# A gated mix of linear attention and a token MLP: phi(q) by token rows, normalised on GpSimd and VectorE and turned by DMA, with six y tiles held

## The chip, the core and the metric

The kernel runs on one core of one Trainium2 chip. TensorE (PE in the profile) multiplies matrices, ScalarE (ACT), VectorE (DVE) and GpSimd (POOL) do the rest, and SyncE (SP) issues nearly all DMAs, in order, from one queue. Times are microseconds of device time of one launch, and the metric is the median over runs.

## What is computed

Inputs are bf16. x has 2048 tokens of 512 features, there are 32 heads of 16, and F is 1792.

```python
def _A_ref(x, wqkv, wo):                      # linear attention
    q, k, v = ...                             # (x @ wqkv), by head
    phi = lambda t: jnp.where(t > 0, t + 1, jnp.exp(t)) + 1e-6
    pq, pk = phi(q), phi(k)
    kv = jnp.einsum("bhsd,bhse->bhde", pk, v)
    z = jnp.einsum("bhsd->bhd", pk)
    num = jnp.einsum("bhqd,bhde->bhqe", pq, kv)
    den = jnp.einsum("bhqd,bhd->bhq", pq, z)[..., None] + 1e-6
    o = num / den
    return ... @ wo                           # heads side by side again

def _B_ref(x, w1, b1, w2, b2):                # MLP over the tokens
    h = _layernorm(x, axis=-1)
    u = _gelu(jnp.einsum("bsd,sf->bdf", h, w1) + b1)
    y = jnp.einsum("bdf,fs->bds", u, w2) + b2
    return ...                                # turned back to (tokens, features)

g = _sigmoid((x * gate_w).sum(-1, keepdims=True))
return g * _A_ref(A_x, A_wqkv, A_wo) + (1 - g) * _B_ref(B_x, ...)
```

The kernel uses A_x for both halves.

## The kernel before

Tokens lie in 16 tiles of 128 (t), features in 4 blocks of 128 (j or k), F in 14 blocks, and tokens also in 4 chunks of 512 (c). A matmul takes a 128x128 block as weights and a 128x512 block as data, into one of the eight PSUM banks of the tag "bank". The helpers mm and load (lines 73 and 126) hold every matmul and every DMA in program order on its engine, and pin does so for the others. In the profile all matmuls therefore have line 75 and all SP DMAs line 127.

The stages, in TensorE's order:

- accA: the first seven F blocks of x normalised times w1, while x and w1 come in and VectorE does the layer norm. gelu goes to ScalarE.
- kacc and Gps: k by token tile, phi(k) as pk, and G = x^T phi(k), which stands for kv before v's weights are applied. SP has loaded xT, x turned, with 16 DMA transposes (line 155). VectorE adds up zacc, the sum of phi(k) over 16 rows of each partition's tokens, split into z_hi and z_lo in bf16.
- The block loop (line 438), b = 0 to 6: each block has sixteen accB matmuls for one of the other seven F blocks. Block 0 then has kv_blocks and z_cols, which sums z over the partitions with eight matmuls of one column and lays it out by head in Z32. Block 1 has w2_blocks, which joins kv and wo to W2sb. Blocks 0 to 3 end with 3, 4, 4 and 5 q groups (line 352): each makes phi(q) turned, features on the partitions and 512 tokens along the row, straight into pqT. The gelus of blocks 0 to 3 run after the last phi; four accB banks are held until then. After block 3 VectorE has the last four gate sums, and after block 4 comes den (line 416): 16 matmuls of pqT by Z32, a reciprocal of 128x512 on VectorE, a store to rd_dram.
- Then SP reads 1/den back 16 times, repeated over each head's 16 rows (rex, line 500), and VectorE multiplies pqT by it in place (line 502). load_w2(1), the second half of w2 in two DMAs, is issued behind those reads. The first half, load_w2(0), was issued before the block loop.
- y and a: a y tile is 14 matmuls of w2 by uT for one token tile. An a tile is 4 matmuls of pqT by W2sb. ScalarE scales a to ga (line 480, three buffers), VectorE adds c1 times y to it into ot (line 489, four buffers), and SP stores ot. The first HOLD = 4 y tiles are all made before the first a tile, and wait in their banks. Tiles 0 to 7 read the first half of w2 and tiles 8 to 15 the second.

phi is one exp on ScalarE and two instructions on VectorE (lines 289 to 301).

Of the kernel before, what the change touches and what calls it, by code (L numbers as in the profile page):

```python
# [8 lines left out]
ACT = mybir.ActivationFunctionType  # L9
ALU = mybir.AluOpType  # L10
AX = mybir.AxisListType
BF16 = mybir.dt.bfloat16
FP32 = mybir.dt.float32
# [3 lines left out]
def kernel(  # L17
# [13 lines left out]
    nc = tc.nc  # L31
    P = nc.NUM_PARTITIONS
    EPS = 1e-5
    PHI_EPS = 1e-6
    DEN_EPS = 1e-6
    HEAD = 16
# [3 lines left out]
    S, D = X.shape  # L40
    F = B_w1.shape[1]
    NT = S // P
    ND = D // P
    NF = F // P
    SC = 512
    NSC = S // SC
# [16 lines left out]
    work = ctx.enter_context(tc.tile_pool(name="work", bufs=3))  # L63
    dpool = ctx.enter_context(tc.tile_pool(name="dpool", bufs=1, space=bass.MemoryType.DRAM))
    psum = ctx.enter_context(tc.tile_pool(name="psum", bufs=8, space=bass.MemoryType.PSUM))

    def ptile(shape, dt, name):
        return persist.tile(shape, dt, name=name, tag=name)

    def bank(name):  # L70
        return psum.tile([P, SC], FP32, name=name, tag="bank")

    def mm(o, lhsT, rhs, start, stop, **kw):
        tc.keep_in_program_order(
            nc.tensor.matmul(o, lhsT=lhsT, rhs=rhs, start=start, stop=stop, **kw)  # L75
        )

    xr = ptile([P, NT, D], BF16, "xr")
    xh = ptile([P, NT, D], BF16, "xh")
    xT = ptile([P, ND, S], BF16, "xT")  # L80
    wq_sb = ptile([P, ND, D], BF16, "wq_sb")
# [3 lines left out]
    pqT = ptile([P, ND, S], BF16, "pqT")  # L85
    uT = ptile([P, NF, D], BF16, "uT")
    G_sb = ptile([P, ND, D], BF16, "G_sb")
    kvbdT = ptile([P, ND, P], BF16, "kvbdT")
    Z32 = ptile([P, ND, 32], BF16, "Z32")
    W2sb = ptile([P, ND, D], BF16, "W2sb")  # L90
    mask = ptile([P, P], BF16, "mask")
    maskH = ptile([P, 8], BF16, "maskH")
    ident = ptile([P, P], BF16, "ident")
    gw_b = ptile([P, D], BF16, "gw_b")
    b_rows = ptile([NF + NT, P], BF16, "b_rows")
# [8 lines left out]
    c1 = ptile([P, NT], FP32, "c1")  # L104
    c2 = ptile([P, NT], FP32, "c2")
    warm = ptile([P, 256], BF16, "warm")
    ones1 = ptile([P, 1], BF16, "ones1")
    zacc = ptile([P, D], FP32, "zacc")
    z_hi = ptile([P, D], BF16, "z_hi")
    z_lo = ptile([P, D], BF16, "z_lo")  # L110
    zcol_sb = ptile([P, ND], FP32, "zcol_sb")
    rden_sb = ptile([P, SC], BF16, "rden_sb")
    eps_t = ptile([P, 1], FP32, "eps_t")
    den_eps_t = ptile([P, 1], FP32, "den_eps_t")
    den_sb = ptile([P, SC], FP32, "den_sb")

    nc.vector.memset(warm[:], 1.0)
    nc.vector.memset(eps_t[:], EPS)
# [5 lines left out]
    pin = tc.keep_in_program_order  # L124

    def load(o, i, eng=None, **kw):
        pin((eng or nc.sync).dma_start(out=o, in_=i, **kw))  # L127
# [24 lines left out]
    for c in range(NSC):  # L152
        for j in range(ND):
# [3 lines left out]
                transpose=True,  # L157
# [6 lines left out]
    for j in range(ND):  # L164
# [10 lines left out]
        out=mask[:], in_=mask[:], compare_op=ALU.is_gt, fill=1.0,  # L175
        base=1 - HEAD, pattern=[[-HEAD, 8], [0, HEAD]], channel_multiplier=1,
    )
    nc.gpsimd.affine_select(
        out=mask[:], in_=mask[:], compare_op=ALU.is_ge, fill=0.0,
        base=0, pattern=[[-HEAD, 8], [0, HEAD]], channel_multiplier=1,  # L180
    )
    nc.gpsimd.memset(maskH[:], 0.0)
    nc.gpsimd.affine_select(
        out=maskH[:], in_=maskH[:], compare_op=ALU.is_gt, fill=1.0,
        base=1 - HEAD, pattern=[[-HEAD, 8]], channel_multiplier=1,
    )
    nc.gpsimd.affine_select(
        out=maskH[:], in_=maskH[:], compare_op=ALU.is_ge, fill=0.0,
        base=0, pattern=[[-HEAD, 8]], channel_multiplier=1,
    )  # L190
    nc.gpsimd.memset(Z32[:], 0.0)
    nc.gpsimd.memset(ones1[:], 1.0)
    nc.gpsimd.memset(den_eps_t[:], DEN_EPS)


    warm_ps = bank("warm_ps")
# [55 lines left out]
    def gate(t):  # L252
        junk = work.tile([P, D], BF16, name="junk", tag="junk", bufs=2)
        tc.keep_in_program_order(
            nc.vector.tensor_tensor_reduce(  # L255
                out=junk[:], in0=xr[:, t, :], in1=gw_b[:], scale=1.0, scalar=0.0,
                op0=ALU.mult, op1=ALU.add, accum_out=gpre[:, t : t + 1],
            )
        )

    GATE_A = 12
# [27 lines left out]
    def phi(o, acc):  # L289
        e = work.tile([P, SC], BF16, name="e", tag="e", bufs=4)  # L290
        pin(nc.scalar.activation(out=e[:], in_=acc[:], func=ACT.Exp))  # L291
        pin(
            nc.vector.tensor_scalar(  # L293
                out=e[:], in0=e[:], scalar1=1.0, scalar2=PHI_EPS, op0=ALU.min, op1=ALU.add
            )
        )
        pin(
            nc.vector.scalar_tensor_tensor(  # L298
                out=o, in0=acc[:], scalar=0.0, in1=e[:], op0=ALU.max, op1=ALU.add
            )  # L300
        )
# [44 lines left out]
    def mlp1_block(j):  # L346
        acc = bank("accB")
        for t in range(NT):
            mlp1(acc, w1B, (j - NFA) * P, t, t == NT - 1)
        return acc  # L350

    def q_group(c, j):
        qacc = bank("qacc")
        for k in range(ND):
            mm(qacc[:], wq_sb[:, k, j * P : (j + 1) * P], xT[:, k, c * SC : (c + 1) * SC],
               k == 0, k == ND - 1)
        phi(pqT[:, j, c * SC : (c + 1) * SC], qacc)

    def z_cols():
        zcol_ps = bank("zcol_ps")  # L360
        for j in range(ND):
            mm(zcol_ps[:, j : j + 1], z_hi[:, j * P : (j + 1) * P], ones1[:], True, False)
            mm(zcol_ps[:, j : j + 1], z_lo[:, j * P : (j + 1) * P], ones1[:], False, True)
        pin(nc.vector.tensor_copy(out=zcol_sb[:], in_=zcol_ps[:, :ND]))
        for j in range(ND):
            pin(
                nc.vector.tensor_scalar_mul(
                    out=Z32[:, j, 8 * j : 8 * j + 8], in0=maskH[:], scalar1=zcol_sb[:, j : j + 1]
                )
            )  # L370

    def kv_blocks():
        kvps = bank("kvps")
# [18 lines left out]
    def w2_blocks():  # L392
        w2ps = [bank("w2ps") for _ in range(ND)]
        for j in range(ND):
            for p in range(0, P, 32):
                r = (p + 32 * j) % P
                mm(w2ps[j][p : p + 32, :], kvbdT[r : r + 32, j, p : p + 32],
                   wo_sb[r : r + 32, j, :], True, True, tile_position=(r, p))
        for j in range(ND):
            evict(W2sb[:, j, :], w2ps[j][:], j)  # L400
# [10 lines left out]
    load_w2(0)  # L411


    rd_dram = dpool.tile([P, SC], BF16, name="rd_dram", tag="rd_dram")

    def den():
        denps = bank("denps")
        for j in range(ND):
            for c in range(NSC):
                mm(denps[32 * c : 32 * c + 32, :], Z32[:, j, :], pqT[:, j, c * SC : (c + 1) * SC],  # L420
                   j == 0, j == ND - 1, tile_position=(0, 32 * c))
        pin(
            nc.scalar.activation(
                out=den_sb[:], in_=denps[:], func=ACT.Identity, bias=den_eps_t[:], scale=1.0
            )
        )
        with nc.allow_low_precision(reason="1/den in bf16 as the operands of the product"):
            pin(nc.vector.reciprocal(out=rden_sb[:], in_=den_sb[:]))
        load(rd_dram[:], rden_sb[:])

    QB = 4
    qlist = [(c, j) for c in range(NSC) for j in range(ND)]
    n_q = [3, 4, 4, 5]
    qi = 0
    waiting = []
    for b in range(NFA):
        acc = mlp1_block(NFA + b)
        waiting.append((acc, NFA + b))  # L440
        if b == 0:
            kv_blocks()
            z_cols()
        if b == 1:
            w2_blocks()
        if b < QB:
            for _ in range(n_q[b]):
                q_group(*qlist[qi])
                qi += 1
        if b >= QB - 1:  # L450
            for a, j in waiting:
                gelu(a, j)
            waiting = []
        if b == QB - 1:
            for t in range(GATE_A, NT):
                gate(t)
        if b == QB:
            den()
    assert qi == len(qlist)


    pin(nc.scalar.activation(out=gth[:], in_=gpre[:], func=ACT.Tanh, scale=0.5))
# [30 lines left out]
        )  # L493
        load(o_view[:, t, d0:d1], ot[:, d0:d1])

    for c in range(NSC):
        for j in range(ND):
            rex = work.tile([P, SC], BF16, name="rex", tag="rex", bufs=8)
            r_src = rd_dram[32 * c + 8 * j : 32 * c + 8 * j + 8, :]
            load(rex[:], r_src.unsqueeze(1).to_broadcast([8, HEAD, SC]))  # L500
            pin(
                nc.vector.tensor_tensor(  # L502
                    out=pqT[:, j, c * SC : (c + 1) * SC],
                    in0=pqT[:, j, c * SC : (c + 1) * SC], in1=rex[:], op=ALU.mult,
                )
            )

    load_w2(1)

    HOLD = 4  # L510
    held = []
    for t in range(HOLD):
        yps = bank("yps")
        y_mm(yps, t, 0, D)
        held.append(yps)
    for t in range(HOLD):
        ga = a_mm(t)
        finish(t, held[t], ga, 0, D)
    for t in range(HOLD, NT):
        ga = a_mm(t)  # L520
# [39 lines left out]
```

## Time and profile before

| | |
|---|---|
| median of 3 runs | 165.72 us (165.0 to 166.07) |
| the profiled execution | 165.5 us, of it a span of 163.8 us from the first instruction to the last |
| granted TensorE clock | 1.000 of full |
| q groups (qacc) on PE | 62.68 to 87.26 us, between the accB blocks |
| y and a tiles on PE | from 98.55 us to the end |
| DVE waits for ACT's exp (line 293) | 7.6 us in 3 times, the longest 3.1 |
| DVE's ot (line 489) waits for an output store | 7.0 us, once |
| first rex product (line 502) to the last, on DVE | 100.97 to 113.76 us |

The profile names a group of instructions by line, engine, operation and tiles (written tile <- read tiles), with the shapes. The timeline merges instructions of one kind that follow one another, with the start, the length, and the number. An idle time stands in brackets with what ended it. Matmuls overlap: one of 128x512 is shown as 379 ns long, but they start 216 ns apart.

### The profile page before, as it was taken

Reading aid. Unit: us, or ns where it says so; the run is one execution under the profiler, and the core shown is the slowest. Engines: PE = TensorE matmul, PEld = TensorE weight load, DVE = VectorE, ACT = ScalarE, POOL = GpSimd, SP = SyncE. Lnnn points to the kernel's source line nnn. Section 1 sums busy time; section 2 is a strip of 40 time slices with the busy share of each in tenths; the row PEclk is TensorE's granted clock in tenths of the full one; section 3 lists DMA queues with packets and bytes.
Section 4 is the critical chain, followed back from the end, with each engine's and each line's share of the span. In section 5 each row is a group of like instructions: output and inputs, shape, how many; then the busy total and the mean of one; then the engine's idle time right before and its main releaser. Section 6 shows DMA issues by size and latency. Waiting matters only on the chain.

```text
span 163.8 us, 2188 instructions
## 1 busy us (share of the span) xinstructions
PE 158.3 (97%) x792; PEld 73.3 (45%) x807; DVE 97.3 (59%) x236; ACT 51.9 (32%) x87; POOL 2.0 (1%) x15
## 2 busy tenths in 40 slices
PE   6899999999999999999999999999999999999992
PEld 4344444444444445444444344444444444444452
DVE  3879989789999996992839743655405111111112
ACT  3220137863233123261438611006312222111110
POOL 4000000000000000000000000000000000000000
PEclk9999999999999999999999999999999999999999
DMA  4899997445999499600000003559992000111001
GB/s 119 278 360 369 363 153 160 96 98 101 327 387 361 95 367 388 255 2 0 0 0 0 4 32 123 182 184 318 400 326 74 32 32 32 43 54 35 32 32 32
DMA packets 26182, 25.57 MB, mean 156 GB/s; under 512 B 10044, under 2 KB 22588, under 8 KB 26172
## 3 DMA queue, kind: packets, MB, share of 16 engines
q1 hardware_dynamic: 26112, 25.43, 49.8%
q8 instruction: 6, 0.10, 0.3%
q14 instruction: 4, 0.03, 0.1%
q10 hardware_dynamic: 60, 0.01, 0.0%
HBM read 21.11 MB, written 2.23 MB: 142 GB/s over the span
## 4 chain that ended last, share of the span: by engine, by line
PE 94%; DMA 2%; issue 1%; SPq 1%; DVE 0%
PE yps L75 29%; PE accA L75 15%; PE accB L75 15%; PE kacc L75 9%; PE qacc L75 8%; PE aps L75 8%; PE Gps L75 8%; DMA w1A<-in_B_w_dram 2%; PE denps L75 1%; SPq L127 1%; PE kvps L75 0%; PE w2ps L75 0%; DVE ot L489 0%; PE zcol_ps L75 0%
## 5 line engine op out<-in xcount | busy, mean ns | idle before, releaser
L75 PE MATMUL yps<-uT,w2h 128*128 128x512 bf16 (+2 forms) x234 | 50.3, 366 | 0.2
L75 PEld LDWEIGHTS <-w2h 128*128 128x128 bf16 x238 | 22.8, 98 | 25.9
L489 DVE SCALAR_TENSOR_TENSOR ot<-yps,c,ga 128x512 bf16<-128x512 f32 (+2 forms) x17 | 11.9, 717 | 35.8 <-PE yps L75 27.5
L480 ACT ACTIVATE ga<-aps,c,gg 128x512 f32<-128x512 f32 x16 | 12.3, 777 | 46.8 <-PE aps L75 46.3
L75 PE MATMUL accA<-xh,w1A 128*128 128x512 bf16 x110 | 25.1, 388 | 0.5 <-DMA w1A<-in_B_w_dram 0.4
L75 PE MATMUL accB<-xh,w1B 128*128 128x512 bf16 x110 | 24.9, 379 | 0.2 <-issue 0.2
L75 PEld LDWEIGHTS <-w1A 128*128 128x128 bf16 x112 | 11.1, 100 | 14.1 <-issue 1.1
L75 PEld LDWEIGHTS <-w1B 128*128 128x128 bf16 x112 | 10.9, 98 | 13.4 <-issue 0.4
L75 PE MATMUL kacc<-wk_sb,xT 128*128 128x512 bf16 x63 | 15.7, 379 | 0.1
L75 PE MATMUL aps<-W2sb,pqT 128*128 128x512 bf16 x62 | 15.7, 379 | 0.1
L75 PE MATMUL Gps<-pk,xr 128*128 128x512 bf16 x62 | 15.5, 379 | 0.1
L291 ACT ACTIVATE e<-qacc 128x512 bf16<-128x512 f32 x16 | 9.6, 597 | 15.5 <-PE qacc L75 14.7
L75 PE MATMUL qacc<-xT,wq_sb 128*128 128x512 bf16 x62 | 14.2, 379 | 0.1
L293 DVE TENSOR_SCALAR e<-e 128x512 bf16<-128x512 bf16 x32 | 9.2, 288 | 8.0 <-ACT e L291 7.6
L291 ACT ACTIVATE e<-kacc 128x512 bf16<-128x512 f32 x16 | 9.2, 598 | 12.7 <-DVE pk L298 6.8
L207 DVE BATCH_NORM_STATS2 stats<-xr 128x6 f32<-128x512 bf16 x16 | 10.7, 671 | 3.6 <-DMA xr<-in_A_x_dram 3.6
L298 DVE SCALAR_TENSOR_TENSOR pk<-kacc,e 128x512 bf16<-128x512 f32 x16 | 11.1, 692 | 1.0
L298 DVE SCALAR_TENSOR_TENSOR pqT<-qacc,e 128x512 bf16<-128x512 f32 x16 | 11.1, 692 | 0.6
L502 DVE TENSOR_TENSOR pqT<-pqT,rex 128x512 bf16<-128x512 bf16 x16 | 6.8, 425 | 6.9 <-DMA rex<-rd_dram 6.9
L255 DVE CUSTOM_DVE_ANT_0 junk<-xr,gw_b 128x512 bf16<-128x512 bf16 x16 | 9.9, 684 | 0.0
L318 DVE TENSOR_TENSOR zacc<-zacc,pk 128x512 f32<-128x512 f32 x14 | 9.6, 684 | 0.1
L75 PEld LDWEIGHTS <-xr 128*128 128x128 bf16 x64 | 6.3, 98 | 7.5
(65 smaller groups left out, 77.4 us busy)
## 6 DMA issues: line engine op xcount, KB each, us to landing
w2h<-in_B_w_dram SPq DMA_DIRECT2D x4, 1792.0 KB
w1A<-in_B_w_dram SPq DMA_DIRECT2D x16, 224.0 KB
w1B<-in_B_w_dram SPq DMA_DIRECT2D x4, 896.0 KB
rex<-rd_dram SPq DMA_DIRECT2D x16, 128.0 KB
out_dram<-ot SPq DMA_DIRECT2D x15, 128.0 KB
xr<-in_A_x_dram SPq DMA_DIRECT2D x5, 256.0 KB
xr<-in_A_x_dram SPq DMA_DIRECT2D x6, 128.0 KB
wk_sb<-in_A_wqkv_dram SPq DMA_DIRECT2D x1, 512.0 KB
```

Source lines behind the costliest of these rows:

```text
L75: nc.tensor.matmul(o, lhsT=lhsT, rhs=rhs, start=start, stop=stop, **kw)
L127: pin((eng or nc.sync).dma_start(out=o, in_=i, **kw))
L207: pin(nc.vector.bn_stats(out=stats[t][:], in_=xr[:, t, :]))
L255: nc.vector.tensor_tensor_reduce(out=junk[:], in0=xr[:, t, :], in1=gw_b[:], scale=1.0, scalar=0.0, op0=ALU.mult, op1=ALU.add, accum_out=gp ...
L291: pin(nc.scalar.activation(out=e[:], in_=acc[:], func=ACT.Exp))
L293: nc.vector.tensor_scalar(out=e[:], in0=e[:], scalar1=1.0, scalar2=PHI_EPS, op0=ALU.min, op1=ALU.add)
L298: nc.vector.scalar_tensor_tensor(out=o, in0=acc[:], scalar=0.0, in1=e[:], op0=ALU.max, op1=ALU.add)
L318: nc.vector.tensor_tensor(out=zacc[:], in0=pks[0][:] if t == 1 else zacc[:], in1=pks[t][:], op=ALU.add)
L480: nc.scalar.activation(out=ga[:], in_=aps[:], func=ACT.Identity, scale=gg[:, t : t + 1], bias=c2[:, t : t + 1])
L489: nc.vector.scalar_tensor_tensor(out=ot[:, d0:d1], in0=yps[:, d0:d1], scalar=c1[:, t : t + 1], in1=ga[:, d0:d1], op0=ALU.mult, op1=ALU.add,)
L502: nc.vector.tensor_tensor(out=pqT[:, j, c * SC : (c + 1) * SC], in0=pqT[:, j, c * SC : (c + 1) * SC], in1=rex[:], op=ALU.mult,)
```

## The change

phi(q) is made with tokens on the partitions: q_tile(t) takes xT as weights and wq as data, and writes phi(q) into xr, whose x is no longer needed by then. z_row sums z with two matmuls by a 128x128 block of ones, so that every partition holds the whole row, and ScalarE copies it to zb. For each tile GpSimd multiplies phi(q) by zb into one of six prod buffers, in which each head has a 17th column that holds 1e-6. VectorE sums each head's 17 columns (den), takes the reciprocal (rd) and multiplies phi(q) by it in place. SP stores the tile to q_dram, and after every fourth tile loads pqT for 512 tokens back with four DMA transposes. den, rd_dram, rex, Z32 and their products go. The last four gates move into blocks 1 and 2, in front of one normalise in each; the other fourteen normalises follow the last block in program order, ahead of load_w2(1). HOLD is 6.

```diff
-    Z32 = ptile([P, ND, 32], BF16, "Z32")
+    zb = ptile([P, D], FP32, "zb")
+    NH = D // HEAD
+    prods = [ptile([P, NH, HEAD + 1], FP32, f"prod{i}") for i in range(6)]
...
+    nc.gpsimd.memset(ones[:], 1.0)
+    for p in prods:
+        nc.gpsimd.memset(p[:, :, HEAD : HEAD + 1], DEN_EPS)
...
-    def q_group(c, j):
+    pq = xr
+    def by_head(a):
+        return a.rearrange("p (h e) -> p h e", e=HEAD)
+
+    def q_tile(t):
         qacc = bank("qacc")
         for k in range(ND):
-            mm(qacc[:], wq_sb[:, k, j * P : (j + 1) * P], xT[:, k, c * SC : (c + 1) * SC],
-               k == 0, k == ND - 1)
-        phi(pqT[:, j, c * SC : (c + 1) * SC], qacc)
-    def z_cols():
...
+            mm(qacc[:], xT[:, k, t * P : (t + 1) * P], wq_sb[:, k, :], k == 0, k == ND - 1)
+        phi(pq[:, t, :], qacc)
+
+    def product(t):
+        prod = prods[t % len(prods)]
+        pin(
+            nc.gpsimd.tensor_tensor(
+                out=prod[:, :, 0:HEAD], in0=by_head(pq[:, t, :]), in1=by_head(zb[:]), op=ALU.mult
+            )
+        )
+
+    def z_row():
+        zps = bank("zps")
+        mm(zps[:], ones[:], z_hi[:], True, False)
+        mm(zps[:], ones[:], z_lo[:], False, True)
+        pin(nc.scalar.copy(out=zb[:], in_=zps[:]))
+
+    q_dram = dpool.tile([S, D], BF16, name="q_dram", tag="q_dram")
+
+    def normalise(t):
+        heads = by_head(pq[:, t, :])
+        prod = prods[t % len(prods)]
+        den = work.tile([P, NH], FP32, name="den", tag="den", bufs=2)
+        pin(nc.vector.tensor_reduce(out=den[:], in_=prod[:], op=ALU.add, axis=AX.X))
+        if t + len(prods) < NT:
+            product(t + len(prods))
+        rd = work.tile([P, NH], FP32, name="rd", tag="rd", bufs=2)
+        pin(nc.vector.reciprocal(out=rd[:], in_=den[:]))
+        pin(
+            nc.vector.tensor_tensor(
+                out=heads, in0=heads,
+                in1=rd[:].unsqueeze(2).to_broadcast([P, NH, HEAD]), op=ALU.mult,
+            )
+        )
+        load(q_dram[t * P : (t + 1) * P, :], pq[:, t, :])
+        if t % 4 == 3:
+            c = t // 4
+            for j in range(ND):
+                load(
+                    pqT[:, j, c * SC : (c + 1) * SC],
+                    q_dram[c * SC : (c + 1) * SC, j * P : (j + 1) * P],
+                    transpose=True,
                 )
...
-    rd_dram = dpool.tile([P, SC], BF16, name="rd_dram", tag="rd_dram")
-    def den():
...
     n_q = [3, 4, 4, 5]
-    qi = 0
+    gates = [[], [12, 13], [14, 15], []]
+    n_norm = [0, 1, 1, 0]
+    qi = ni = 0
...
         if b == 0:
             kv_blocks()
-            z_cols()
+            z_row()
...
         if b < QB:
             for _ in range(n_q[b]):
-                q_group(*qlist[qi])
+                q_tile(qi)
+                if qi < len(prods):
+                    product(qi)
                 qi += 1
+            for t in gates[b]:
+                gate(t)
+            for _ in range(n_norm[b]):
+                normalise(ni)
+                ni += 1
         if b >= QB - 1:
             for a, j in waiting:
                 gelu(a, j)
             waiting = []
-        if b == QB - 1:
-            for t in range(GATE_A, NT):
-                gate(t)
-        if b == QB:
-            den()
-    assert qi == len(qlist)
+    assert qi == NT
+    while ni < NT:
+        normalise(ni)
+        ni += 1
...
-    for c in range(NSC):
-        for j in range(ND):
-            rex = work.tile([P, SC], BF16, name="rex", tag="rex", bufs=8)
-            r_src = rd_dram[32 * c + 8 * j : 32 * c + 8 * j + 8, :]
-            load(rex[:], r_src.unsqueeze(1).to_broadcast([8, HEAD, SC]))
...
     load_w2(1)

-    HOLD = 4
+    HOLD = 6
```

More of the change, by code (lines that the diff above doesn't have):

```diff
@@ L88 @@
     kvbdT = ptile([P, ND, P], BF16, "kvbdT")
-    Z32 = ptile([P, ND, 32], BF16, "Z32")
+    zb = ptile([P, D], FP32, "zb")
+    NH = D // HEAD
+    prods = [ptile([P, NH, HEAD + 1], FP32, f"prod{i}") for i in range(6)]
     W2sb = ptile([P, ND, D], BF16, "W2sb")
     mask = ptile([P, P], BF16, "mask")
-    maskH = ptile([P, 8], BF16, "maskH")
     ident = ptile([P, P], BF16, "ident")
@@ L106 @@
     warm = ptile([P, 256], BF16, "warm")
-    ones1 = ptile([P, 1], BF16, "ones1")
+    ones = ptile([P, P], BF16, "ones")
     zacc = ptile([P, D], FP32, "zacc")
@@ L110 @@
     z_lo = ptile([P, D], BF16, "z_lo")
-    zcol_sb = ptile([P, ND], FP32, "zcol_sb")
-    rden_sb = ptile([P, SC], BF16, "rden_sb")
     eps_t = ptile([P, 1], FP32, "eps_t")
-    den_eps_t = ptile([P, 1], FP32, "den_eps_t")
-    den_sb = ptile([P, SC], FP32, "den_sb")
     nc.vector.memset(warm[:], 1.0)
@@ L181 @@
     )
[L182 to L193, printed above, removed]
+    nc.gpsimd.memset(ones[:], 1.0)
+    for p in prods:
+        nc.gpsimd.memset(p[:, :, HEAD : HEAD + 1], DEN_EPS)
     warm_ps = bank("warm_ps")
@@ L350, in mlp1_block @@
         return acc
-    def q_group(c, j):
+    pq = xr
+    def by_head(a):
+        return a.rearrange("p (h e) -> p h e", e=HEAD)
+    def q_tile(t):
         qacc = bank("qacc")
         for k in range(ND):
-            mm(qacc[:], wq_sb[:, k, j * P : (j + 1) * P], xT[:, k, c * SC : (c + 1) * SC],
-               k == 0, k == ND - 1)
-        phi(pqT[:, j, c * SC : (c + 1) * SC], qacc)
-    def z_cols():
-        zcol_ps = bank("zcol_ps")
-        for j in range(ND):
[L362 to L368, printed above, removed]
+            mm(qacc[:], xT[:, k, t * P : (t + 1) * P], wq_sb[:, k, :], k == 0, k == ND - 1)
+        phi(pq[:, t, :], qacc)
@@ L369, in z_cols @@
                 )
-            )
     def kv_blocks():
@@ L411 @@
     load_w2(0)
-    rd_dram = dpool.tile([P, SC], BF16, name="rd_dram", tag="rd_dram")
-    def den():
-        denps = bank("denps")
-        for j in range(ND):
-            for c in range(NSC):
[L420 to L429, printed above, removed]
     QB = 4
-    qlist = [(c, j) for c in range(NSC) for j in range(ND)]
     n_q = [3, 4, 4, 5]
-    qi = 0
+    gates = [[], [12, 13], [14, 15], []]
+    n_norm = [0, 1, 1, 0]
+    qi = ni = 0
     waiting = []
@@ L494, in finish @@
         load(o_view[:, t, d0:d1], ot[:, d0:d1])
-    for c in range(NSC):
-        for j in range(ND):
-            rex = work.tile([P, SC], BF16, name="rex", tag="rex", bufs=8)
-            r_src = rd_dram[32 * c + 8 * j : 32 * c + 8 * j + 8, :]
-            load(rex[:], r_src.unsqueeze(1).to_broadcast([8, HEAD, SC]))
[L501 to L506, printed above, removed]
     load_w2(1)
-    HOLD = 4
+    HOLD = 6
     held = []
```

## The prediction

> **What bounds the kernel now.** I read the page's busy times and its chain first.
>
> ```profile
> PE 158.3 (97%) x792; PEld 73.3 (45%) x807; DVE 97.3 (59%) x236; ACT 51.9 (32%) x87; POOL 2.0 (1%) x15
> ...
> PE 94%; DMA 2%; issue 1%; SPq 1%; DVE 0%
> ```
>
> TensorE (PE) is busy 97% of the span and carries 94% of the chain. So only two things move the time: matmuls that disappear, and waits that are put in front of matmuls. Next is the matmul stream, first around the part that goes, then around the second half of the y tiles (timeline of PE; start, length, what).
>
> ```profile
> 90.65 1.05 PE L75 MATMUL denps<-pqT,Z 128*32 128x512 bf16 x16
> ...
> 91.85 6.85 PE L75 MATMUL accB<-xh,w1B 128*128 128x512 bf16 x31 [0.16 <-issue]
> ...
> 129.62 1.03 PE L75 MATMUL aps<-W2sb,pqT 128*128 128x512 bf16 x4
> 130.49 3.19 PE L75 MATMUL yps<-uT,w2h 128*128 128x512 bf16 x14
> ```
>
> The last line is tile 8, the first that reads the second half of w2. Its 14 matmuls take 3.02 us (the next group starts at 133.51). That half is loaded by two DMAs that SP issues, so the third view is SP's own queue in order of time.
>
> ```profile
> 17.86 21.40 SPq L127 DMA_TRANSPOSE xT<-in_A_x_dram  x16
> ...
> 55.50 0.39 SPq L127 DMA_DIRECT2D wq_sb<-in_A_wqkv_dram  x1
> 56.00 1.05 SPq L127 DMA_DIRECT2D w2h<-in_B_w_dram  x2
> 96.20 0.35 SPq L127 DMA_DIRECT2D rd_dram<-rden_sb  x1
> 97.93 10.99 SPq L127 DMA_DIRECT2D rex<-rd_dram  x16
> 109.01 1.03 SPq L127 DMA_DIRECT2D w2h<-in_B_w_dram  x2
> 114.45 47.22 SPq L127 DMA_DIRECT2D out_dram<-ot  x17
> ```
>
> Three things are to be seen. A transpose holds SP for 21.40/16 = 1.34 us, and the row by tile gives the single ones:
>
> ```profile
> L127 SPq DMA_TRANSPOSE xT<-in_A_x_dram x16: 1213/1259/1875, 17.9 to 38.0; - x16
> ```
>
> From the issue of a store to DRAM to the first read of what it stored pass 97.93 - 96.20 = 1.73 us. And w2's second half leaves at 109.01, behind all 16 rex reads. How long such a load takes shows at its first half, issued at 56.00 (stretches of 2 us; the last column is GB/s):
>
> ```profile
> 65.00:67.00 2.00, 2.00 (x11) 0.89 (x10) 1.79 (x11) 0.60 (x1) 0.00 (x0) 1.00 1.05 388
> 67.00:69.00 2.00, 2.00 (x25) 0.76 (x24) 1.93 (x5) 0.00 (x0) 0.00 (x0) 1.00 0.66 235
> ```
>
> 0.47 MB remain after 67.00, 1.2 us at 388 GB/s: the data end at 68.2, 12.2 us after the issue, with wq's 0.5 MB in front. Now it is hidden: 109.0 + 12.2 = 121.2, tile 8 starts at 130.49. This slack of 9 us is what the change works on.
>
> **The change, TensorE.** The den matmuls go: 91.85 - 90.72 (end of the accB group in the chain) = 1.13 us. The eight z matmuls go (62.24 to 62.45, 0.21 us), two 128x512 ones come (2 x 0.216 = 0.43 us). The q matmuls swap operands and stay 64 of the same size. Net -0.9 us. Six held y tiles in place of four only reorder: before tile 8 there are still y 0 to 7 and a 0 to 8. So undisturbed, tile 8 starts at 129.6, and its eighth matmul, which needs the second of the two w2 DMAs, at 129.6 + 1.5 = 131.1. Eight banks for six y and two a tiles: the third a tile waits for the first ga (0.78 us); PE has 0.86 us of the second a tile in between, so a bubble of some 0.2 us, which I set at nothing because the wait below swallows it.
>
> **Rows, ScalarE, VectorE, GpSimd.** ACT gets one copy of 0.59 us (the rate of its G_sb casts) ahead of the first exp, in a 4.8 us idle time. One normalise on VectorE has three instructions, of which no row shows any exactly. The sum over 128x544 f32: the f32 addition of 512 takes 684 ns, so 0.73 us. The reciprocal of 32: 147 ns for one element, 3354 for 512, so 6.29 ns each, 0.34 us. The product with a broadcast f32: between 425 ns (all bf16) and 684 (f32), I take 0.69. Dependent instructions start 0.04 us after one another, independent ones overlap by 0.08: 1.76 us a tile (bounds 1.4 and 2.5, the latter if sharing with GpSimd doubles the product). Two gates (0.61 each) and one normalise, 2.98 us, go into blocks 1 and 2 where VectorE now waits 3.11 us for exp: hidden, with 0.1 us of cover in block 2, and 1.0 in block 1, as 0.87 us of z work has gone. What is queued behind them is the next block's phi, and PE's q banks behind that; the fifth q group of block 3 has 0.9 us until the first one's bank is needed. The new wait, the sum on GpSimd's product: products 0 to 5 are ready long before; later ones are asked for six tiles ahead, and eight of them (8 to 15) fall in the tail. GpSimd shows a one-input pass over 128x128 in 0.34 us, so 1.4 us for 512 columns and up to 2.7 with two inputs. It would set the pace only above 3.2.
>
> **SP's queue decides.** The 16 rex reads (10.99 us) go; 16 stores and 16 transposes come, all ahead of w2's second half. VectorE ends the last phi at 89.3 (89.2 now), and normalise 3 at 89.3 + 2 x 1.76 = 92.8. The first transpose starts 1.73 us after that store, at 94.5; four hold SP for 4 x 1.34 = 5.35, to 99.9. Each later group of four waits behind them: three stores at 0.4 us, 1.73 us from the fourth store to the transposes, 5.35 us: 8.3 us. That is longer than VectorE's 4 x 1.76 = 7.0, so SP sets the pace and its cover is gone: 99.9 + 3 x 8.3 = 124.8, where w2's second half leaves. Now it leaves at 109.0. Data end 12.2 us later, at 137.0; I add 1.0 for the landing to be seen (0 to 1.9: the output stores behind the present load have their bytes through near 121.5 and free their reader at 123.38). So 138.0 against 131.1: TensorE waits 6.9 us, in two pieces, for the first half of the load at tile 8's start and for the second at its eighth matmul. The first output stores lie behind the same load; with four ot buffers the fifth finish waits for them, as it now waits 7.0 us. Held then are four y banks, one a bank whose ga lacks a buffer, and three more, so it costs nothing until a tile 9, up to 2 us if a bank is given out earlier. Sum: -0.9 + 6.9 = +6.0 us. The profiled run took 165.5 (span 163.8), 0.2 below the median of 165.72: 171.5 for it, 171.7 for the median.
>
> All terms at their low ends (transposes at 1.21, stores at 0.33 and 1.4, normalise at 1.4, load at 10.9, no landing) send the load off at 120.4: 0.2 us of wait, 165.0. At their high ends (normalise 2.5 for tiles 2 and 3, a group of 9.5 because stores queue behind transposes that still move, landing 1.0) it leaves at 130.5: 177.4.
>
> The Trainium skill (DMA: Bandwidth & Descriptors, section Latency and other measured facts) gives 261 GB/s for a DMA transpose, an estimated 0.5 us for 128 KB. By it the load would leave at about 117.7 and the wait would be gone, -0.9 us. The row above, 1259 ns or 104 GB/s for just this shape, speaks against it.
>
> The granted clock is full in all 40 slices, and the longest idle time of PE that the trace shows is 1.3 us. TensorE: Matmul & The Clock Gate (Part 1, What's actually happening) halves the clock after an idle window of some 3.4 us; an estimate by it is 1.7 us more. No row here shows it.
>
> **The rivals.**
> Not slower: SP passes a group faster, because one group of four transposes isn't held as 16 in a row are. For: the transposes at 17.86 share the DMA queues with w1's data. Against: the shortest of 16 is still 1.213 us, and DMA was at half share by 30 us. It decides when the load leaves before 131.1 - 13.2 = 117.9; SP then follows VectorE (last normalise 89.3 + 14 x 1.76 = 113.9, store to transpose 1.73), which leaves 2.3 us for the last four transposes, 0.57 each. Result 165.72 - 0.9 = 164.8.
>
> Much slower: VectorE or GpSimd sets the pace. At 2.5 us a normalise the last ends at 89.3 + 35 = 124.3, the load leaves at 131.4 and is there at 144.6: -0.9 + 13.5 = 12.6, 178.3. GpSimd at 4 us a product gives much the same: 90.0 + 8 x 4 + 1.1 = 123.1, 177.1. For it: both engines read SBUF at once and no row shows that. Against: GpSimd has 1.2 us of room at the dearer bound.
>
> The change not doing what it says is no rival of weight: the queue's order is written out.
>
> **How the numbers follow.** 1% of the time, 1.66 us, is what a measurement here can tell. The forecast, SP's queue as the pace: 0.68, 171.7, its own range 165.0 to 177.4. Not slower, 164.8: 0.16. Much slower: 0.16, 177 and up. The range, 166.5 to 177.5, leaves out most of the second rival's upper part and of the first. Faster by over 1% needs 1.66 us where only 0.9 us of matmuls go: 0.03. Within 1%: the first rival less that, 0.13, and 0.04 of the forecast's low end, 0.17. Slower: 0.80.
>
> **What would show it.** Right: PE's waits name a DMA of w2h, 6 to 7 us at tile 8, nothing before; SP's transposes in four groups of four near 1.3 us with the w2h issue near 125; accB groups without the den gap. Wrong: the w2h issue before 118 (first rival); DVE's sum waiting on POOL, or normalise over 2.1 us (second); a PE wait in the q blocks (cover of 0.1 us was too thin); matmuls at a lower clock behind the wait. The forecast falls if transposes hold SP for clearly less than 1.2 us.

## The result, and the profile after

The changed kernel takes 177.19 us (median of 6 runs, 175.72 to 178.25) against 165.6 us before: a ratio of 1.0711, 95% interval 1.0677 to 1.0744, or +11.6 us. The forecast was 171.7 us, with a range of 166.5 to 177.5. The direction held, and the range by 0.3 us; the loss is nearly twice what was forecast. Ratios and intervals here and below leave out slow runs, those over 1.5% above the fastest of the same kernel. The profiled execution took 177.2 us with a span of 175.1.

First the page after: busy times, the granted clock by slice, and the chain.

```profile
PE 161.0 (92%) x771; PEld 73.2 (42%) x785; DVE 121.0 (69%) x262; ACT 51.9 (30%) x87; POOL 20.6 (12%) x32
...
PEclk9999999999999999999999999998799969999999
...
PE 48%; DVE 30%; DMA 13%; SPq 4%; issue 2%; ACT 1%; ACTq 0%
```

TensorE's share fell from 97% to 92%, and VectorE now carries 30% of the chain where it carried none. The clock is no longer full everywhere. What the engines waited for stands in the view of waits (total, times, longest):

```profile
DVE ot L502 <- DMA out_dram<-ot: 15.6, 1, 15.6
...
PE yps L75 <- DMA w2h<-in_B_w_dram: 4.7, 2, 3.0
PE aps L75 <- ACT ga L493: 3.4, 1, 3.4
...
PE qacc L75 <- DVE xr L287: 0.8, 1, 0.8
```

The same waits in the timeline of TensorE:

```profile
86.94 1.02 PE L75 MATMUL qacc<-wq_sb,xT 128*128 128x512 bf16 x4 [0.78 <-DVE xr L287]
...
116.35 1.89 PE L75 MATMUL aps<-W2sb,pqT 128*128 128x512 bf16 x8
121.68 5.88 PE L75 MATMUL aps<-W2sb,pqT 128*128 128x512 bf16 x20 [3.44 <-ACT ga L493]
...
137.04 1.69 PE L75 MATMUL yps<-uT,w2h 128*128 128x512 bf16 x7 [1.70 <-DMA w2h<-in_B_w_dram]
141.72 3.17 PE L75 MATMUL yps<-uT,w2h 128*128 128x512 bf16 x7 [3.00 <-DMA w2h<-in_B_w_dram]
```

The last two lines are tile 8, split by its two waits for w2. Seven matmuls take 1.69 us before the second wait and 3.17 behind it. Twenty a matmuls take 5.88 us behind the 3.44 us wait, where 4.5 is usual (20 x 0.216 and 0.16 at the end). The granted clock says why (stretches of 4 us; the third column from the right):

```profile
120.00:124.00 4.00, 2.32 (x6) 0.84 (x6) 2.14 (x6) 1.86 (x3) 0.00 (x0) 0.64 0.55 165
124.00:128.00 4.00, 4.00 (x18) 1.72 (x17) 1.50 (x2) 3.09 (x5) 0.00 (x0) 0.93 0.62 70
...
140.00:144.00 4.00, 2.28 (x6) 0.89 (x7) 1.85 (x3) 1.00 (x2) 0.00 (x0) 0.70 0.64 228
```

So TensorE's account is: 0.9 us of matmuls less, 0.8 + 3.4 + 4.7 us of waits, 1.4 + 1.6 us of matmuls at a lower clock behind two of them. That is 11.0 us, against 11.3 between the spans (175.1 and 163.8).

Where the load of w2 went shows in SP's queue:

```profile
97.21 5.05 SPq L125 DMA_TRANSPOSE pqT<-q_dram  x4
102.30 3.16 SPq L125 DMA_DIRECT2D q_dram<-xr  x4
106.88 5.04 SPq L125 DMA_TRANSPOSE pqT<-q_dram  x4
111.97 2.03 SPq L125 DMA_DIRECT2D q_dram<-xr  x4
115.43 5.04 SPq L125 DMA_TRANSPOSE pqT<-q_dram  x4
120.51 2.04 SPq L125 DMA_DIRECT2D q_dram<-xr  x4
123.97 5.20 SPq L125 DMA_TRANSPOSE pqT<-q_dram  x4
129.22 1.19 SPq L125 DMA_DIRECT2D w2h<-in_B_w_dram  x2
130.44 42.58 SPq L125 DMA_DIRECT2D out_dram<-ot  x17
```

It leaves at 129.22, 20.2 us later than before and 4.4 later than forecast, and its second DMA lets TensorE go on at 141.72, 12.5 us later. The output stores stand behind it, which is the 15.6 us wait of VectorE above. And this, in VectorE's timeline, is one normalise of the tail beside a product of GpSimd (tile 2), and the last instruction of one without (tile 10):

```profile
90.51 0.71 DVE L376 TENSOR_REDUCE den<-prod 128x32 f32<-128x544 f32 x1
91.25 0.35 DVE L380 RECIPROCAL rd<-den 128x32 f32<-128x32 f32 x1
91.64 1.37 DVE L382 TENSOR_TENSOR xr<-xr,rd 128x512 bf16<-128x512 bf16 x1
...
110.98 0.69 DVE L382 TENSOR_TENSOR xr<-xr,rd 128x512 bf16<-128x512 bf16 x1
```

In GpSimd's timeline the product that runs beside the first one:

```profile
91.29 1.17 POOL L357 TENSOR_TENSOR prod<-xr,zb 128x512 f32<-128x512 bf16 x1 [5.88 <-DVE den L376]
```

The sum and the reciprocal cost what was forecast. The product with 1/den takes 0.69 us alone and 1.37 beside GpSimd's product, for the eight tiles of the tail (2 to 9) that have one running. Normalise starts every 2.42 us in these eight tiles, and every 1.74 us behind them. VectorE's product ends at 93.01, 0.55 us after GpSimd's at 92.46; e6 below comes back to that.

### The profile page after: what moved, and what is told of

It reads as the page before. It is cut to its first block, busy times and chain, and to the rows that moved or that the text cites. A ratio compares the mean times of both kernels' runs of the same rounds, so it can differ in the third digit from the quotient of the medians.

```text
span 175.1 us, 2204 instructions
## 1 busy us (share of the span) xinstructions
PE 161.0 (92%) x771; PEld 73.2 (42%) x785; DVE 121.0 (69%) x262; ACT 51.9 (30%) x87; POOL 20.6 (12%) x32
## 4 chain that ended last, share of the span: by engine, by line
PE 48%; DVE 30%; DMA 13%; SPq 4%; issue 2%; ACT 1%; ACTq 0%
PE yps L75 14%; DVE xr L382 10%; PE accA L75 9%; PE kacc L75 8%; PE Gps L75 8%; DMA w2h<-in_B_w_dram 7%; DVE den L376 6%; DVE xr L287 5%; SPq L125 4%; PE accB L75 4%; PE aps L75 4%; DVE rd L380 3%; DMA xr<-in_A_x_dram 3%; DMA w1A<-in_B_w_dram 2%; DVE e L282 2%; DVE junk L244 2%
## 5 line engine op out<-in xcount | busy, mean ns | idle before, releaser
L75 PE MATMUL yps<-uT,w2h 128*128 128x512 bf16 (+2 forms) x233 | 51.4, 374 | 4.9 <-DMA w2h<-in_B_w_dram 4.7
L357 POOL TENSOR_TENSOR prod<-xr,zb 128x512 f32<-128x512 bf16 x16 | 18.6, 1173 | 88.2 <-DVE xr L287 65.5
L75 PE MATMUL aps<-W2sb,pqT 128*128 128x512 bf16 x64 | 17.2, 408 | 3.5 <-ACT ga L493 3.4
L75 PEld LDWEIGHTS <-xT 128*128 128x128 bf16 x128 | 12.4, 98 | 16.1 <-issue 1.3
L382 DVE TENSOR_TENSOR xr<-xr,rd 128x512 bf16<-128x512 bf16 x16 | 17.8, 1113 | 0.6
L75 PE MATMUL qacc<-wq_sb,xT 128*128 128x512 bf16 x62 | 14.5, 379 | 0.9 <-DVE xr L287 0.8
L280 ACT ACTIVATE e<-qacc 128x512 bf16<-128x512 f32 x16 | 9.6, 598 | 11.8 <-PE qacc L75 11.6
L280 ACT ACTIVATE e<-kacc 128x512 bf16<-128x512 f32 x16 | 9.2, 598 | 12.7 <-DVE pk L287 6.8
L75 PEld LDWEIGHTS <-pqT 128*128 128x128 bf16 x64 | 6.7, 104 | 12.7 <-issue 6.4
L287 DVE SCALAR_TENSOR_TENSOR xr<-qacc,e 128x512 bf16<-128x512 f32 x16 | 11.1, 692 | 0.6
L376 DVE TENSOR_REDUCE den<-prod 128x32 f32<-128x544 f32 x16 | 11.3, 708 | 0.0
```

Source lines behind the costliest of these rows:

```text
L287: nc.vector.scalar_tensor_tensor(out=o, in0=acc[:], scalar=0.0, in1=e[:], op0=ALU.max, op1=ALU.add)
L357: nc.gpsimd.tensor_tensor(out=prod[:, :, 0:HEAD], in0=by_head(pq[:, t, :]), in1=by_head(zb[:]), op=ALU.mult)
L376: pin(nc.vector.tensor_reduce(out=den[:], in_=prod[:], op=ALU.add, axis=AX.X))
L382: nc.vector.tensor_tensor(out=heads, in0=heads, in1=rd[:].unsqueeze(2).to_broadcast([P, NH, HEAD]), op=ALU.mult,)
```

## The experiments

The main theory, from here on the queue theory: the loss is w2's second half, queued on SP behind the transposes. Rivals: the gates theory (gg, c1 and c2 stand behind the last normalise on VectorE, and the a tiles wait for them), the hold theory (six held tiles cost banks), and, for the size, contention between GpSimd and VectorE. All runs are compared with the kernel before on the same chip. All but e11 are edits of the changed kernel.

### e1: w2's second half from another queue

```diff
-    load_w2(1)
+    load_w2(1, nc.scalar)
```

> The second half of w2 is issued from ScalarE's queue behind the last gelu, near 99 us, and no longer behind the transposes. Queue theory (tile 8 waits for w2 because SP issues it last): TensorE's two waits at tile 8 go. Tile 8 was reached at 135.2 and its eighth matmul started at 141.7 in place of 136.7, so 5.0 us come back, and 1.6 us of slower matmuls behind the wait: 170.6. What stays is the 3.4 us wait for the first ga. Gates theory (the loss is that gg, c1 and c2 stand behind the last normalise): the tile 8 wait is a consequence only, and 176 to 177 stays. Hold theory (six held tiles cost banks): no change, 177.

Measured: 177.18 us (174.76 to 179.65), spread too wide for an interval, so that no gain can be told. The wait for w2 is gone, but another stands at the same tile:

```profile
PE yps L75 <- DVE ot L502: 4.2, 1, 4.2
```

None of the three expectations had this. VectorE's fifth finish waits 12.7 us for an output store, which now leaves SP at 136.66, again behind the transposes. Tile 8's bank waits for that finish.

The load, whose two DMAs now leave at 98.31 and 109.98, also costs something where it stands. Beside it, single transposes hold SP for up to 2.32 us (1.42 at most in the changed kernel), and SP waits 10.2 us in place of 5.1 for its stores to q_dram to land. The last group of transposes starts 7.6 us later than in the changed kernel (123.97):

```profile
131.59 5.03 SPq L125 DMA_TRANSPOSE pqT<-q_dram  x4
```

### e2 and e3: the gate columns in front, alone and with e1

```diff
     while ni < NT:
         normalise(ni)
         ni += 1
+        if ni == 8:
+            pin(nc.vector.tensor_scalar(out=gg[:], ...))
+            pin(nc.vector.tensor_scalar(out=c1[:], ...))
+            pin(nc.vector.tensor_tensor(out=c2[:], ...))
```

The three lines behind the loop go (not shown), and the tanh on ScalarE that they read moves ahead of it.

> gg, c1 and c2 are computed after normalise 7 in place of behind normalise 15. Queue theory: the wait of 3.4 us at the third a tile goes, but w2 is there no earlier, so the same time is spent waiting at tile 8: 177, within 1. Gates theory: 3.4 us and what follows from it come back, 173 or less.

Measured: 178.08 us, ratio 1.0752 (1.0690 to 1.0813). TensorE's wait for ga went, one of 2.2 us for the first finish came (it still stands behind the last normalise), and the wait for w2 grew from 4.7 to 6.0. The time is the same as the changed kernel's within the intervals. So the gates theory falls as the only cause.

> Both edits. Queue theory: nothing on TensorE's path is left of the change but a wait of 0.8 us in block 3 and the 0.9 us fewer matmuls, so 165.6 within 0.7: the same as before the change. If VectorE's pace mattered for TensorE in another way than through w2 and the gates, 168 or more.

Measured: 174.07 us, ratio 1.0529 (1.0472 to 1.0587). Less, but far from 165.6. What TensorE still waits for:

```profile
PE yps L75 <- DVE ot L501: 3.6, 1, 3.6
PE aps L75 <- DVE ot L501: 2.2, 1, 2.2
...
PE qacc L75 <- DVE xr L287: 0.8, 1, 0.8
```

And SP's queue has the reason for the first line:

```profile
128.35 5.04 SPq L125 DMA_TRANSPOSE pqT<-q_dram  x4
133.43 3.83 SPq L125 DMA_DIRECT2D out_dram<-ot  x6
```

The first output store leaves at 133.43, 12 us after its tile was finished (121.2), since SP has its last transposes to issue. The queue theory was right about the queue and too narrow about what stands in it: not only w2, the output stores too.

### e4: HOLD back to 4

> HOLD 4 in place of 6. Queue theory: the first a tiles come 6 us earlier and wait for gg until 120.9, longer than now, but the work ahead of tile 8 still ends before w2 is there, or just: 177 to 179. Hold theory: four held tiles avoid the loss, 172 or less.

Measured: 176.57 us, ratio 1.0683 (1.0660 to 1.0706). The a tiles come earlier and wait 7.8 us for ga; at tile 8 only 0.4 us are left to wait. The last wait ends with the load of w2 all the same. HOLD isn't the cause.

### e5, e6 and e8: GpSimd beside VectorE

e5 leaves the products of tiles 8 to 15 out, so those tiles are divided by old denominators:

```diff
-        if t + len(prods) < NT:
+        if t + len(prods) < 8:
             product(t + len(prods))
```

> GpSimd's products of tiles 8 to 15 are left out, so the denominators of those tiles are old ones; all else of the changed kernel stays. Contention theory (VectorE's product with 1/den takes 1.37 us in place of 0.69 because GpSimd's product runs beside it): every 1/den product takes 0.69, a normalise 1.74, VectorE's last ends near 114.9 in place of 120.4. SP then sets the pace as the prediction had it, with groups of 8.65 us as the last one measured: the load of w2 leaves at 126.8 in place of 129.2, 174.8. If the length comes from the f32 operand and the broadcast, it stays 1.37 and the time 177.

Measured: 173.84 us, ratio 1.0495 (1.0413 to 1.0577). The row of the 1/den products from 90 to 116 us:

```profile
L382 DVE TENSOR_TENSOR xr<-xr,rd 128x512 bf16<-128x512 bf16 x14 | 9.7, 692 | 0.5
```

All 14 take 0.69 us, so the f32 operand and the broadcast are not what makes them long. The load of w2 leaves at 127.78, 1.0 us later than expected, and yet the time is 1.0 us under the expectation: behind tile 8's second wait, of 1.66 us here, seven matmuls ran at full clock, 1.68 us in place of 3.17.

e6 makes the late products twice:

```diff
         if t + len(prods) < NT:
-            product(t + len(prods))
+            for _ in range(2 if t > 1 else 1):
+                product(t + len(prods))
```

> The products of tiles 8 to 15 are made twice on GpSimd, same result. If VectorE's two-input product is held until GpSimd's instructions are done: it takes 1.37 + 1.16 = 2.5 us for those eight tiles, VectorE ends 9.3 us later, the load of w2 leaves near 138 and the time is 186. If the two engines only share bandwidth while both run, the product stays near 1.4 us and the time between 177 and 179.

Measured: 179.27 us in one run, so only its trace is used. GpSimd is busy without a gap here, and the 1/den products that lie wholly beside it take this long (rows from 94 to 112 us):

```profile
L383 DVE TENSOR_TENSOR xr<-xr,rd 128x512 bf16<-128x512 bf16 x7 | 11.5, 1640 | 0.2
```

Neither 2.5 nor 1.4. The single instructions show what happens. Two products that follow one another on GpSimd:

```profile
94.34 1.16 POOL L357 TENSOR_TENSOR prod<-xr,zb 128x512 f32<-128x512 bf16 x1
95.58 1.50 POOL L357 TENSOR_TENSOR prod<-xr,zb 128x512 f32<-128x512 bf16 x1
```

VectorE's product of that time runs from 94.41 to 96.05 and ends 0.55 us after the first of the two. All seven do, and so do all ten of the changed kernel that meet a product of GpSimd, whatever was left of that when VectorE's started (1.09 us in the case shown, 0.82 in the changed kernel). So the two engines don't share a rate. VectorE's product is held until the one product that runs on GpSimd is done, and not for those queued behind it; the expectation of 2.5 us had it wait for both. GpSimd pays in its turn: the product that follows takes 1.50 us in place of 1.16, and the 16 take 21.57 us.

e8 moves the product in time, with the same work:

```diff
-        if t + len(prods) < NT:
-            product(t + len(prods))
...
+        if t + len(prods) < NT:
+            pin(nc.gpsimd.tensor_copy(out=gate_p[:], in_=pq[:, t, D - 1 : D]))
+            product(t + len(prods))
         load(q_dram[t * P : (t + 1) * P, :], pq[:, t, :])
```

> GpSimd's product of tile t+6 starts after VectorE's 1/den product of tile t (a one-column copy on GpSimd waits for it), so that it runs beside the next tile's sum and reciprocal (0.71 + 0.35 us) and not beside its product. The work is the same. Contention of the two-input product: it takes 0.8 to 1.0 us, a normalise about 2.05, VectorE ends near 117.5, the load of w2 leaves near 127.5, 175.5. If any VectorE instruction is slowed by GpSimd's, the sum takes 1.3 and nothing is gained, 177.

Measured: ratio 1.0521 (1.0400 to 1.0642), resting on two runs, too wide to tell its time from 177; the median of all four is 176.13 us. The trace is clear, from 92 to 108 us:

```profile
L382 DVE TENSOR_TENSOR xr<-xr,rd 128x512 bf16<-128x512 bf16 x8 | 7.4, 926 | 0.3
L378 DVE TENSOR_REDUCE den<-prod 128x32 f32<-128x544 f32 x9 | 6.4, 707 | 0.0
L380 DVE RECIPROCAL rd<-den 128x32 f32<-128x32 f32 x8 | 2.8, 353 | 0.3
```

The sum and the reciprocal run beside GpSimd's product at 0.707 and 0.353 us, as without it. Of the three only the product, which has two SBUF inputs, pays: it starts when GpSimd's has some 0.37 us left in place of 0.82, and again ends 0.55 us after it. The load of w2 leaves at 127.37, as expected.

### e9: no finish waits for a store

```diff
-        ot = work.tile([P, D], BF16, name="ot", tag="ot", bufs=4)
...
-                out=ot[:, d0:d1], in0=yps[:, d0:d1], scalar=c1[:, t : t + 1], in1=ga[:, d0:d1],
+                out=xh[:, t, d0:d1], in0=yps[:, d0:d1], scalar=c1[:, t : t + 1], in1=ga[:, d0:d1],
...
-        load(o_view[:, t, d0:d1], ot[:, d0:d1])
+        load(o_view[:, t, d0:d1], xh[:, t, d0:d1])
```

> As e3_both, and the output tiles go into xh, which is dead by then, in place of four ot buffers, so that no finish waits for an output store that stands behind the transposes on SP. If that wait (11.6 us on VectorE, 3.6 us on TensorE at tile 8, and the slow matmuls behind it) is what e3 lost: the wait goes, 2.2 us at the a tiles (finish behind the last normalise) and 0.8 in block 3 stay, 167.5 to 169. If the load of w2 beside the transposes is what costs, 172 or more.

Measured: 168.92 us, ratio 1.0185 (1.0094 to 1.0276). The wait at tile 8 is gone. What stays is 0.8 us in block 3 and 2.2 at the a tiles, with 1.7 us of slow matmuls behind the latter, less the 0.9 us of matmuls.

### e10, e12 and e13: all edits together, and all but one

e10 is e9 with e8's order and with normalise 1 moved out of block 2 (n_norm = [0, 1, 0, 0]). e12 is e10 without the edit of w2's queue, and e13 is e10 without the edit of the ot buffers.

> As e9_own_ot, with the products in step as in e8 and with normalise 1 moved from block 2 to the tail. If the accounting is right (block 3's wait 0.8, the a tiles' wait 2.2 behind the last normalise and some 1.5 of slow matmuls behind it are all that e9 has left): block 3's wait goes, VectorE's last normalise ends near 117.6, when the first finish is due, and 165.25 - 0.9 + 0 to 1 = 164.4 to 165.4. If the transposes beside the load of w2 bring pqT too late for the fifth a tile, 167 or more.

Measured: 164.1 us, ratio 0.9948 (0.9933 to 0.9963), a little faster than the kernel before. Its page:

```profile
PE 157.0 (97%) x771; PEld 72.6 (45%) x785; DVE 116.8 (72%) x262; ACT 52.1 (32%) x87; POOL 21.9 (14%) x42
```

TensorE is back at 97% with less to do, and its timeline shows no wait from 60 us on. 0.52% of 165.04 is 0.86 us (0.6 to 1.1 by the interval), which is the size of the matmuls that the change took away.

> e10_all with w2's second half back on SP's queue behind the transposes. Queue theory: SP's groups of 8.6 us start at 96.1, the load leaves at 127 and its second DMA has landed 12.5 us later at 139.5; TensorE would want it at 130.2, so 9.3 us of wait and 1.6 of slow matmuls: 175. If e10's gain came from the gates and VectorE's pace, 168 or less.

Measured: 176.94 us, ratio 1.0683 (1.0624 to 1.0741). The load left at 130.82, 3.8 us later than expected, and TensorE waited 9.6 us for it.

> e10_all with the four ot buffers back. The first output store leaves SP at 133.4 behind the last transposes. If finish 4 waits for it and tile 8's bank for that: tile 8 starts near 136.3 as in e3 in place of 128.7, and slow matmuls behind it, 172 to 173.5. If the ot buffers only matter together with a late VectorE, 165.

Measured: 173.54 us, ratio 1.0511 (1.0459 to 1.0564): TensorE waits 6.4 us at tile 8 for a finish that waits for its store.

### e11: HOLD 6 in the kernel before

> The kernel before with HOLD 6 alone. If six held tiles cost only a bubble of some 0.2 us at the third a tile: the same, 165.2 to 165.6. If they cost banks later on, 167 or more.

Measured: 165.19 us, ratio 1.0011 (0.9998 to 1.0024). Six held tiles by themselves cost nothing that shows.

## Why the prediction was right, and what it mis-sized

**Right.** The matmuls that go are worth 0.9 us: e10 shows 0.86 where nothing else is in the way. The mechanism is SP's queue: transposes hold it for 1.26 us each, also in groups of four, and w2's second half comes too late for tile 8. e12 shows that its place in that queue alone is worth some 12 us, against e10 (ratios of 1.0683 and 0.9948). The first rival (a faster group on SP) is out: no transpose took under 1.12 us, and four take 5.05, close to the forecast 5.35. HOLD was rightly set at nothing (e11).

**Right by little.** 177.19 us lies 0.3 us under the top of the range, and also where the second rival began ("177 and up"). The time alone doesn't tell the two apart; the trace does. SP set the pace of two of the three later groups, VectorE that of one, and three of the signs of being wrong were there: a normalise of 2.42 us (over 2.1), the wait in the q blocks, and the lower clock. That the range held is in part luck. The sum for its upper end had neither the second group at VectorE's pace nor the clock in it. And the terms named for that end add up to a load at 129.9 and to 176.8 us, not to 130.5 and 177.4, which is under the measured time; those named for the lower end send the load off at 120.1, not 120.4.

**Mis-sized: the product with 1/den.** The step said 0.69 us, by the f32 row, with 2.5 for a whole normalise as an upper bound if sharing with GpSimd doubled it. Beside GpSimd it takes 1.37. Normalise asks for GpSimd's next product behind its own sum, so that product has 0.82 us left when VectorE's starts, and VectorE's ends 0.55 us after it. e5, without the late products, loses 3.6 us less (ratios of 1.0495 and 1.0711), of which 1.5 are the clock behind tile 8's second wait. The longer product enters the sum three times. In block 2 it is more than the cover, which was given as 0.1 us: block 3's phis end at 90.6 in place of 89.3, and TensorE waits 0.8 us. Normalise 2 and 3 take 1.3 us longer, so that the first transposes start at 97.2, 2.7 later than forecast. And the second group is set by VectorE, 9.67 us for four, where SP was to set it with 8.3. The other two groups are SP's as forecast, but 8.55 us: four stores back to back take 0.5 us each, not 0.4, and from the issue of the last of them to the first transpose pass some 1.9 us, not 1.73. Together the load left 4.4 us late against the forecast; that it then took 12.5 us and not 13.2 gives 0.7 back: 3.7 us.

**Left out of the sum: the lower clock.** Behind tile 8's second wait, of 3.00 us, seven matmuls take 3.17 us in place of 1.69, at a granted clock of 0.70 from 140 to 144 us; with the a tile that follows this costs 1.6 us. The prediction had it beside the sum as an estimate from the Trainium skill (TensorE: Matmul & The Clock Gate, Part 1, What's actually happening), 1.7 us for an idle window of some 3.4 us. The trace agrees with the size, not with the length of the wait. 3.7 and 1.6 are the 5.3 us by which the sum of +6.0 fell short of +11.3 in the profiled run.

**Wrong in detail.** "Nothing before tile 8": with VectorE at 120.4 in place of 113.9, gg, c1 and c2 came late, and the third a tile waited 3.4 us. On the path this costs nothing that e2 shows, because TensorE would only have waited longer at tile 8. The wait for w2 is 4.7 us, not 6 to 7, since the earlier waits had made TensorE late for it. GpSimd's product was bounded by 1.4 and 2.7 us and takes 1.16, under both. The reciprocal's slope is 6.28 ns by its two rows, not 6.29; its 0.34 us stays (measured 0.35).

**What the forecast did not look for.** It named the output stores behind the load and priced them at up to 2 us. They stand behind the transposes as well, and once w2 is out of the way they are the next limit, of about the same size: e1 shows no gain for that reason, and because the load beside the transposes makes these later. e13 loses 9 of the 12.6 us again that e10 gains on the changed kernel. e10 has five edits (w2's queue, the gate columns' place, the ot buffers, the products' time, normalise 1's block). Only the first and the third were taken out of it singly; which of the other three it needs, and what each gives, stays open.

## What to carry to other kernels

A transfer that is put into an in-order DMA queue is paid by everything that stands behind it there. List all of it, with the time at which each is due, as a fix for the first only uncovers the second. A VectorE product of two SBUF operands that meets a GpSimd product is to be costed as ending 0.55 us after that one, so what counts is how much of GpSimd's is left when VectorE's starts. And a wait of TensorE of a few us is to be costed with slower matmuls behind it: 1.4 to 1.9 us behind most such waits here, 2.8 behind one of 5.4 us in e6's one run, and none behind the one of 2.2 us in e3.

## What the runs showed of the hardware

- VectorE's product of two SBUF operands, 0.69 us alone, ended 0.54 to 0.55 us after the GpSimd product that was running when it started: 1.37 us long in the changed kernel (ten of ten), 0.93 in e8, 1.64 in e6. In e6 the GpSimd product that followed took 1.50 us in place of 1.16.
- phi's middle step, with one bf16 SBUF input, was held as well: where it met a GpSimd product it ended 0.15 us after that and took 0.52 to 0.62 us in the changed kernel, in place of 0.28. The sum over 544 f32 (0.71), the reciprocal of 32 (0.35) and phi's last step with one operand in PSUM (0.69) kept their times.
- A DMA transpose of 512x128 bf16 held SP for 1.12 to 1.42 us in the changed kernel, in groups of four, with a median of 1.26 as in the row of 16 before. Beside the load of w2 (e1) single ones held it for up to 2.32 us.
- TensorE's clock fell behind waits of 3.4 and 3.0 us. Behind a wait of 2.2 us it fell in e9 (0.62 from 122 to 126 us) and stayed full in e3. So the length of one wait does not settle it here, and neither does the idle window of some 3.4 us that the Trainium skill gives (the section named above).
